# Two or four of twelve gate blocks by seven products instead of eight, in seven of nine chunks

## The chip, the cores and the metric

The kernel runs on one core of a Trainium2 chip. The metric is device time in microseconds from the first to the last instruction of the program and what lies around it. Three runs of the kernel before gave 318.49 us in the median (318.02 to 319.49). The core's engines work side by side, each through its own queue in program order: TensorE (PE), which multiplies and writes into the eight banks of PSUM; VectorE (DVE) and ScalarE (ACT), which read PSUM and SBUF; GpSimd (POOL), which here works on SBUF alone; and SyncE (SP), which issues most transfers.

## The reference

Windowed attention (8 batches, 8 heads, 576 tokens, head size 64; four heads with a plain window of 32, four with a dilated one), and behind it a block with gates:

```python
attn = softmax(where(mask[h], q @ k.T / 8, -1e9))      # per batch and head
x = (attn @ v), transposed to [8 * 576, 8 * 64]        # 4608 tokens x 512
g = x @ w_gate                                         # 512 x 1536
gelu = 0.5 * g * (1 + erf(g / sqrt(2)))
out = (gelu * (x @ w_val)) @ w_out                     # 1536 x 512
```

Inputs and output are float32.

## The kernel before

**Tiling.** The block behind the attention runs over 9 chunks of 512 tokens (`run_chunk`, c = 0 to 8). Each chunk has two stages. In the *gate stage* the 1536 middle columns are 12 blocks of 128 (nb = 0 to 11). For each block TensorE makes a gate and a value: four matmuls each (128 rows of weights from `wg` or `wv`, 512 tokens of `xT`, one for each quarter of the 512 inputs; `ffn1_part`, L622) into one bank each. ScalarE makes the Gelu of the gate bank (`g`, L905), VectorE multiplies it with the value bank into `u_all` (the word `u`, L910). In the *output stage* `u_all` is multiplied with `w_out`. There, from chunk 1 on, a 2 x 2 scheme of seven products replaces eight (`products`, L704): the 12 blocks form six pairs, `wx` holds sums of `w_out`, and `u_sums` (L665, L670, L672; the words `k`) makes sums of u on VectorE: the first sum `@0` of a pair, from the two blocks, is needed by products 7 and 5, the second sum `@1` by product 6, the third sum `@2`, in place in `u_all`, by product 3. The products run in the order 1, 7, 6, 4, 5, 2, 3, twelve matmuls of 256 columns each, on two banks; `part_out` (the words `q`, L729, L738, L742) saves a bank between two products in `snap` (two parts of `vdiag`, and `turned`), or adds a saved one and sends it to `out`.

**Attention between.** The attention of the batch that the next chunk needs is laid between the products of the output stage of chunks 0 to 6: scores S (L457), exponentials P on ScalarE (L487), masks M on VectorE (L492), denominators D, logarithm and exponential l and r on ScalarE (L584, L590; tags `lg` and `rb`), numerators N and the division X on VectorE into `xT` (L613). GpSimd turns incoming float32 rows of q, k and v into float16 (L216, L228, L253).

**Order.** Nothing is scheduled automatically: each chunk's program is a string of words that `gate_words` and `out_words` make and `run_program` reads. A number emits so many matmuls of the stage's list, `g` and `u` the Gelu and the product of a block, `k`, `q`, `S`, `M` and so on the steps above. The order of the words is the order in each engine's queue. `gate_banks` gives a block its two banks: from chunk 2 on blocks of even number have (0, 7), those of odd number (1, 4).

## Time and profile before

| | us |
|---|---|
| median of three runs | 318.49 |
| the profiled execution | 318.54 |
| its span, first to last instruction | 316.8 |
| TensorE busy | 310.3 |
| VectorE busy | 211.6 |
| ScalarE busy | 163.0 |
| GpSimd busy | 84.5 |

The chunks begin at 18.5 (0), 55.3 (1), 88.4 (2), 121.9 (3), 155.3 (4), 188.2 (5), 221.0 (6), 253.4 (7) and 283.4 us (8). A row of the chain of waits has a start, a length, and the engine, the tile and the line that the time goes to. A row of groups has the line, the engine, the operation with the tiles that it writes and reads, their shapes and how often; then the busy time and the mean in ns of one; then the idle time ahead of them and who ended it. A row of stages has the stretch, its length, and for each engine the busy time and the instructions; then the granted clock (1.00 is full), the share of the DMA engines, and GB/s.

### The profile page before, as it was taken

The page shows a single profiled execution, that of the slowest core. Times are in us where ns is not written, and L with a number is a line of the kernel's source. Part 1 is how long each engine was busy: PE and PEld are TensorE (multiplying, and loading weights), DVE is VectorE, ACT ScalarE, POOL GpSimd, SP SyncE. Part 2 cuts the span into 40 slices and gives each one's busy share as a digit, 9 for nine tenths or more (in the row PEclk, how much of TensorE's full clock was granted, in tenths as well). Part 3 has the DMA queues.
Part 4 walks back from the last instruction along what each step waited for, and adds up shares of the span by engine and source line. Part 5 has one row for each costly group of instructions (what it writes and reads, how often), then busy time and mean ns, then how long its engine had stood idle before and what let it go on. Part 6 is the DMA issues. An engine that isn't in the chain of part 4 may idle for free.

```text
span 316.8 us, 8447 instructions
## 1 busy us (share of the span) xinstructions
PE 310.3 (98%) x3489; PEld 183.8 (58%) x3489; DVE 211.6 (67%) x368; ACT 163.0 (51%) x247; POOL 84.5 (27%) x134
## 2 busy tenths in 40 slices
...
PEclk9999999999999999999999999999999999999999
...
GB/s 187 185 200 206 206 198 149 257 204 197 160 262 154 198 241 147 246 206 195 160 239 247 158 187 177 244 167 131 35 0 2 79 59 1 0 107 27 0 2 132
DMA packets 110790, 47.15 MB, mean 149 GB/s; under 512 B 83616, under 2 KB 110240, under 8 KB 110752
## 3 DMA queue, kind: packets, MB, share of 16 engines
...
q8 instruction: 27, 0.44, 0.6%
...
HBM read 37.75 MB, written 9.44 MB: 149 GB/s over the span
## 4 chain that ended last, share of the span: by engine, by line
PE 93%; DVE 2%; DMA 2%; ACT 1%; issue 0%; POOL 0%; DVEq 0%
PE ps L622 59%; PE ps L704 23%; PE ps L457 6%; PE ps L629 3%; DMA xT<-in_q_dram 2%; PE ps L377 1%; ACT P L487 1%; DVE xT L613 0%; DVE P L492 0%; PE ps L796 0%; PE ps L446 0%; PE ps L397 0%; DVE u_all L910 0%; ACT rb L590 0%; POOL band L122 0%
## 5 line engine op out<-in xcount | busy, mean ns | idle before, releaser
L905 ACT ACTIVATE g<-ps 128x512 f16<-128x512 f32 x108 | 64.4, 597 | 103.1 <-PE ps L622 100.8
L910 DVE SCALAR_TENSOR_TENSOR u_all<-g,ps 128x512 f16<-128x512 f16 x108 | 73.8, 685 | 63.6 <-PE ps L622 49.0
L622 PE MATMUL ps<-xT,wv 128*128 128x512 f16 x432 | 112.3, 379 | 0.0
L622 PE MATMUL ps<-xT,wg 128*128 128x512 f16 x432 | 111.4, 379 | 0.2 <-DMA wg<-in_moe_w_gate_dram 0.2
L622 PEld LDWEIGHTS <-wg 128*128 128x128 f16 x432 | 42.1, 98 | 50.1 <-DMA wg<-in_moe_w_gate_dram 0.2
L622 PEld LDWEIGHTS <-wv 128*128 128x128 f16 x432 | 42.3, 98 | 49.6 <-issue 0.2
L704 PEld LDWEIGHTS <-u_all 128*128 128x128 f16 x390 | 36.7, 98 | 6.5 <-issue 0.3
L704 PE MATMUL ps<-wx,ux 128*128 128x256 f16 x288 | 35.4, 273 | 0.1
L704 PE MATMUL ps<-wo,u_all 128*128 128x256 f16 (+1 forms) x294 | 35.2, 271 | 0.0
L613 DVE TENSOR_TENSOR xT<-ps,rb 128x576 f16<-128x576 f32 x32 | 29.1, 938 | 4.5 <-PE ps L457 3.6
L487 ACT ACTIVATE P<-ps 128x832 f16<-128x832 f32 (+1 forms) x32 | 25.3, 835 | 11.4 <-PE ps L457 11.3
L216 POOL CAST s<-stage 128x640 f16<-128x640 f32 x24 | 18.3, 790 | 46.1 <-DMA stage<-in_q_dram 32.5
L704 PEld LDWEIGHTS <-ux 128*128 128x128 f16 x288 | 27.7, 98 | 4.1 <-issue 0.2
L253 POOL CAST v<-stage 128x1152 f16<-128x1152 f32 x11 | 12.7, 1152 | 62.7 <-DMA stage<-in_v_dram 47.5
L665 DVE TENSOR_TENSOR ux<-u_all 128x512 f16<-128x512 f16 x48 | 24.4, 509 | 1.7
L584 ACT ACTIVATE lg<-ps 128x576 f32<-128x576 f32 x30 | 18.8, 655 | 6.9 <-PE ps L457 3.7
L590 ACT ACTIVATE rb<-lg 128x576 f32<-128x576 f32 x30 | 19.0, 688 | 0.1
L228 POOL CAST s<-stage 128x512 f16<-128x512 f32 x24 | 15.4, 670 | 9.8 <-DMA stage<-in_q_dram 8.1
L672 DVE TENSOR_TENSOR u_all<-ux,u_all 128x512 f16<-128x512 f16 (+1 forms) x32 | 13.8, 430 | 0.9
L670 DVE TENSOR_TENSOR ux<-u_all,ux 128x512 f16<-128x512 f16 (+1 forms) x32 | 13.5, 422 | 1.1
L729 DVE SCALAR_TENSOR_TENSOR part<-ps,vdiag 128x512 f32<-128x512 f32 x15 | 10.3, 688 | 3.7 <-PE ps L704 3.7
L704 PE MATMUL ps<-wx,u_all 128*128 128x256 f16 x96 | 11.8, 273 | 0.0
...
## 6 DMA issues: line engine op xcount, KB each, us to landing
...
```

What stands on the lines that cost most here:

```text
L216: nc.gpsimd.tensor_copy(s16[:, 1280 * t + 640 * g : 1280 * t + 640 * g + 640].rearrange("p (k c) -> p k c", k=5), st_of(i).rearrange("p (k ...
L228: nc.gpsimd.tensor_copy(s16[:, at : at + 512].rearrange("p (r h d) -> p h r d", r=4, h=2), st_of(i)[:, 512 * g : 512 * g + 512].rearrange( ...
L457: nc.tensor.matmul(o[cols], lhs[rows], rhs[rows], start=st, stop=end, skip_group_check=True)
L487: nc.scalar.activation(pt[:, 0 : src.shape[1]], src, AF.Exp, bias=0.0, scale=scale)
L584: nc.scalar.activation(lg, psf[:, c0 : c0 + S], AF.Ln)
L590: nc.scalar.activation(rb, tiles.pop(("lg", n)), AF.Exp, scale=-1.0)
L613: nc.vector.tensor_tensor(dst, num, rb, ALU.mult)
L622: nc.tensor.matmul(ps[:, bank, :], w[:, kc, ns], xT[kc][:, tok], start=first, stop=end)
L665: nc.vector.tensor_tensor(ux[:, j, 0:2], k0, u_all[:, 2 * j : 2 * j + 2, hi], ALU.subtract)
L704: lambda o=o, s=s[:, P * p : P * p + P], t=t[:, c0:c1], st=st, end=end: nc.tensor.matmul(o, s, t, start=st, stop=end, skip_group_check=True)
L905: nc.scalar.activation(g, ps[:, gate_banks(c, args[0])[0], :], AF.Gelu)
L910: nc.vector.scalar_tensor_tensor(u_all[:, nb, :], tiles.pop(("g", nb)), -USCALE if c in SEVEN and nb % 2 else USCALE, val, ALU.mult, ALU.mult)
```

## The change

In chunks 3 to 8 the blocks 2 and 3 (pair 1), and in chunks 7 and 8 also the blocks 4 and 5 (pair 2), are no longer made by four matmuls for each gate and value. The product of the pair's 256 weight columns with 512 tokens over 512 inputs is cut into 2 x 2 quarters of weights and of x, and made by seven products of quarters (`ffn1_seven`, the words `f`). One product has four matmuls of 256 columns: gate and value, two blocks of 128 inputs each. Gate and value share one bank, 256 columns each.

- **Sums of weights** (`gate_sums`, words `h`): four sums each for gate and value; for pair 1 in chunk 2 on VectorE, for pair 2 in chunk 6 on GpSimd. They lie in columns of x that are no longer needed.
- **Sums of x** (`x_sums`, words `x`): four of 128 x 512 per chunk; for chunks 3 to 5 on VectorE at the start of the gate stage, for 6 to 8 on GpSimd. For this `xT` becomes one tile.
- **Out of the banks** (`quarter_out`): after products 1, 6 and 7 ScalarE copies the bank into a saved one; after 2, 5 and 4 VectorE adds a saved one to the bank, into a float32 quarter of 128 x 512 (in buffers of `rb` and `lg`); after 3 ScalarE copies. Two words later ScalarE makes the Gelu of the quarter's gate half (`quarter_gelu`), and another word later VectorE the product (`quarter_u`), 128 x 256 each.
- **Places.** The products stand one by one between the half blocks of four matmuls of the direct blocks 4 to 9 (in chunks 7 and 8 those of both pairs, from block 6 on). Pair 1 uses banks 1 and 4, pair 2 banks 2 and 3. The direct blocks in between all use banks 0 and 7, in chunks 7 and 8 also 5 and 6.
- **Sums of u**, in chunks 1 to 8: the second and third sums of pair 4 are made together with those of pair 5; in the output stage of chunks 1 to 6 the third sum moves behind the first two masks. In chunks 3 to 8 pair 1's sums come late in the gate stage.

Three places on VectorE. The first is chunk 4's gate stage from its start (`ux` takes a first or second sum of u, `ps` are the banks). Before:

```order
L910 SCALAR_TENSOR_TENSOR u_all<-g,ps 128x512 x2
L665 TENSOR_TENSOR ux<-u_all 128x512
L910 SCALAR_TENSOR_TENSOR u_all<-g,ps 128x512 x2
L665 TENSOR_TENSOR ux<-u_all 128x512
L670 TENSOR_TENSOR ux<-u_all,ux 128x2x256
L672 TENSOR_TENSOR u_all<-ux,u_all 128x2x256
L910 SCALAR_TENSOR_TENSOR u_all<-g,ps 128x512 x2
```

Now:

```order
L670 TENSOR_TENSOR xT<-xT 128x512 x4
L1017 SCALAR_TENSOR_TENSOR u_all<-g,ps 128x512 x3
L709 TENSOR_TENSOR quarter<-ps,vdiag 128x512
L766 TENSOR_TENSOR ux<-u_all 128x512
L1017 SCALAR_TENSOR_TENSOR u_all<-g,ps 128x512
L766 TENSOR_TENSOR ux<-u_all 128x512
L1017 SCALAR_TENSOR_TENSOR u_all<-g,ps 128x512
L726 SCALAR_TENSOR_TENSOR u_all<-g,quarter 128x256
L709 TENSOR_TENSOR quarter<-ps,turned 128x512
L1017 SCALAR_TENSOR_TENSOR u_all<-g,ps 128x512
L709 TENSOR_TENSOR quarter<-ps,vdiag 128x512
```

Four sums of x stand ahead of the first u, and adds of banks and half-width u between the direct ones. The second place is the end of chunk 4's gate stage and the first masks. Before:

```order
L910 SCALAR_TENSOR_TENSOR u_all<-g,ps 128x512 x2
L665 TENSOR_TENSOR ux<-u_all 128x512
L670 TENSOR_TENSOR ux<-u_all,ux 128x256
L742 TENSOR_SCALAR vdiag<-ps 128x512
L672 TENSOR_TENSOR u_all<-ux,u_all 128x256
L492 TENSOR_TENSOR P_2975<-P_2975,two_p 128x832
L492 TENSOR_TENSOR P_2977<-P_2977,two_p 128x832
```

Now:

```order
L1017 SCALAR_TENSOR_TENSOR u_all<-g,ps 128x512
L771 TENSOR_TENSOR ux<-u_all,ux 128x2x256
L1017 SCALAR_TENSOR_TENSOR u_all<-g,ps 128x512
L766 TENSOR_TENSOR ux<-u_all 128x512
L771 TENSOR_TENSOR ux<-u_all,ux 128x2x256
L843 TENSOR_SCALAR vdiag<-ps 128x512
L493 TENSOR_TENSOR P_3037<-P_3037,two_p 128x832
L493 TENSOR_TENSOR P_3039<-P_3039,two_p 128x832
L773 TENSOR_TENSOR u_all<-ux,u_all 128x2x256 x2
```

A second sum (of pairs 0 and 1) stands between the last two u, the second sum ahead of the saved bank is twice as wide, and the third sums stand behind the masks. The third place is the end of chunk 7's gate stage. Before:

```order
L665 TENSOR_TENSOR ux<-u_all 128x512
L670 TENSOR_TENSOR ux<-u_all,ux 128x256
L672 TENSOR_TENSOR u_all<-ux,u_all 128x256
L910 SCALAR_TENSOR_TENSOR u_all<-g,ps 128x512 x2
L665 TENSOR_TENSOR ux<-u_all 128x512
L670 TENSOR_TENSOR ux<-u_all,ux 128x256
L672 TENSOR_TENSOR u_all<-ux,u_all 128x256
```

Now:

```order
L726 SCALAR_TENSOR_TENSOR u_all<-g,quarter 128x256 x3
L1017 SCALAR_TENSOR_TENSOR u_all<-g,ps 128x512
L726 SCALAR_TENSOR_TENSOR u_all<-g,quarter 128x256
L766 TENSOR_TENSOR ux<-u_all 128x512
L726 SCALAR_TENSOR_TENSOR u_all<-g,quarter 128x256
L766 TENSOR_TENSOR ux<-u_all 128x512 x2
L1017 SCALAR_TENSOR_TENSOR u_all<-g,ps 128x512
L771 TENSOR_TENSOR ux<-u_all,ux 128x3x256
L1017 SCALAR_TENSOR_TENSOR u_all<-g,ps 128x512
L766 TENSOR_TENSOR ux<-u_all 128x512
```

Five half-width u and two more first sums have moved in ahead of the last two u. The core of the diff:

```diff
@@ -78,7 +78,8 @@
     wg_t = [const.tile([P, NKC, b - a], F16, tag=f"wg{i}", name=f"wg{i}") for i, (a, b) in enumerate(WC)]
     wv_t = [const.tile([P, NKC, b - a], F16, tag=f"wv{i}", name=f"wv{i}") for i, (a, b) in enumerate(WC)]
     wo_t = [const.tile([P, 4, DM], F16, tag=f"wo{i}", name=f"wo{i}") for i in range(3)]
-    xT = [const.tile([P, NT], F16, tag=f"xT{i}", name=f"xT{i}") for i in range(NKC)]
+    x_all = const.tile([P, NKC, NT], F16, tag="xT", name="xT")
+    xT = [x_all[:, i] for i in range(NKC)]
 
     vraw = [const.tile([P, 4 * NB2 * D], F16, tag=f"v{i}", name=f"v{i}") for i in range(3)]
     vdiag = const.tile([P, 2 * NB2 * P], F16, tag="vdiag")
@@ -624,6 +625,106 @@
     def parts_of(order):
         return [(kc, i == 0, i == len(order) - 1) for i, kc in enumerate(order)]
 
+    ONE = ((1, (1, 4)),)
+    IN_PLACES = {c: ONE if c < 7 else ONE + ((2, (2, 3)),) for c in range(3, NCH)}
+    IN_SEVEN = {c: [j for j, _ in IN_PLACES[c]] for c in IN_PLACES}
+    sums_at = {1: 0, 2: 2 * CH, 3: 3 * CH}
+    free_pool = range(6, NCH)
+    def sums_of(j, s):
+        return x_all[:, s, sums_at[j] : sums_at[j] + CH].rearrange("p (m k n) -> p m k n", m=2, k=2)
...
+    def gate_sums(j, part):
+        for m in range(2):
+            (a11, a12), (a21, a22) = quarters(j, m)
+            s1, s2, s3, s4 = (sums_of(j, s)[:, m] for s in range(4))
+            out_, first, other, op = (
+                (s1, a21, a22, ALU.add),
+                (s2, s1, a11, ALU.subtract),
+                (s3, a11, a21, ALU.subtract),
+                (s4, a12, s2, ALU.subtract),
+            )[part]
+            (nc.vector if j == 1 else nc.gpsimd).tensor_tensor(out_, first, other, op)
+    def x_halves(c):
+        at = [slice(c * CH + 2 * P * h, c * CH + 2 * P * h + 2 * P) for h in range(2)]
+        return [[x_all[:, 2 * k : 2 * k + 2, a] for a in at] for k in range(2)]
+    def x_sum(s):
+        return x_all[:, s, CH : 2 * CH].rearrange("p (k t) -> p k t", k=2)
+    def x_sums(c):
+        (b11, b12), (b21, b22) = x_halves(c)
+        t1, t2, t3, t4 = (x_sum(s) for s in range(4))
+        for out_, first, other in ((t2, b12, b11), (t1, b22, t2), (t3, b22, b12), (t4, b21, t1)):
+            (nc.gpsimd if c in free_pool else nc.vector).tensor_tensor(out_, first, other, ALU.subtract)
+    def ffn1_seven(c, j, kind, bank, first):
+        (b11, b12), (b21, b22) = x_halves(c)
+        for m in range(2):
+            (a11, a12), (_, a22) = quarters(j, m)
+            s1, s2, s3, s4 = (sums_of(j, s)[:, m] for s in range(4))
+            left, right = {
+                1: (a11, b11),
+                2: (a12, b21),
+                3: (s4, b22),
+                4: (a22, x_sum(3)),
+                5: (s1, x_sum(1)),
+                6: (s2, x_sum(0)),
+                7: (s3, x_sum(2)),
+            }[kind]
+            for k in range(2):
+                nc.tensor.matmul(
+                    ps[:, bank, 2 * P * m : 2 * P * m + 2 * P],
+                    left[:, k],
+                    right[:, k],
+                    start=first and m == 0 and k == 0,
+                    stop=k == 1,
+                    skip_group_check=True,
+                )
+    def quarter_out(c, j, kind, bank):
+        src, kept = ps[:, bank, :], {1: 0, 6: 1, 7: 2}.get(kind)
+        saved = snap if bank in (1, 4) else [stage[:, DM * i : DM * i + DM] for i in range(3)]
+        if kept is not None:
+            nc.scalar.copy(saved[kept], src)
+            return
+        n = tiles["quarters"] = tiles.get("quarters", 0) + 1
+        t = nrm.tile([P, S], F32, tag=("rb", "lg", "rb", "lg", "rb")[n % 5], bufs=(3, 2, 3, 2, 3)[n % 5], name="quarter")[:, 0:DM]
+        if kind == 3:
+            nc.scalar.copy(t, src)
+        else:
+            nc.vector.tensor_tensor(t, src, saved[{2: 0, 4: 1, 5: 2}[kind]], ALU.add)
+        nb, half = 2 * j + (kind in (4, 5)), int(kind in (3, 5))
+        tiles.setdefault("ready", []).append((nb, half, t))
+    def quarter_gelu():
+        for nb, half, t in tiles.pop("due", []):
+            g = ffn.tile([P, 2 * P], F16, tag="gq")
+            nc.scalar.activation(g, t[:, 0 : 2 * P], AF.Gelu)
+            tiles.setdefault("gated", []).append((nb, half, t, g))
+        tiles["due"] = tiles.pop("ready", [])
+    def quarter_u():
+        for nb, half, t, g in tiles.pop("gated", []):
+            dst = u_all[:, nb, 2 * P * half : 2 * P * half + 2 * P]
+            by = -USCALE if nb % 2 else USCALE
+            nc.vector.scalar_tensor_tensor(dst, g, by, t[:, 2 * P : 4 * P], ALU.mult, ALU.mult)
...
@@ -850,6 +951,12 @@
 
         if c == 0:
             return ((4, 5), (6, 7))[nb] if nb < 2 else ((0, 1), (2, 3))[nb % 2]
+        if c in IN_SEVEN:
+            if nb in (1, 11):
+                return (1, 4)
+            if c > 6:
+                return (5, 6) if nb % 2 else (0, 7)
+            return (4, 1) if nb == 9 else (0, 7)
         return ((0, 7), (1, 6) if c == 1 else (1, 4))[nb % 2]
 
...
@@ -864,7 +971,7 @@
                 first.append((nb, gi, (kc, i == 1, i == NKC)))
         else:
             first = [(nb, gi, part) for nb in range(2) for gi in range(2) for part in parts_of(range(NKC))]
-        order = [(nb, gi) for nb in range(2, NNB) for gi in range(2)]
+        order = [(nb, gi) for nb in range(2, NNB) if nb // 2 not in IN_SEVEN.get(c, ()) for gi in range(2)]
         if c == 0:
             order = [(nb + n, gi) for nb in range(2, 10, 2) for gi in range(2) for n in range(2)] + order[16:]
         rest = [(nb, gi, part) for nb, gi in order for part in parts_of(range(NKC))]
@@ -915,6 +1022,19 @@
                 u_sums(*args)
             elif kind == "K":
                 weight_sums(*args)
+            elif kind == "f":
+                j, product, place = args
+                ffn1_seven(c, j, product, place, product in (1, 2, 7))
+                quarter_u()
+                quarter_gelu()
+                quarter_out(c, j, product, place)
...
             elif kind == "q":
                 what, eng, at = (args + [c])[:3]
                 part_out(at, what, eng, out_banks(at)[what in (1, 3, 5)])
@@ -952,21 +1072,59 @@
         sums = [""] * NNB
         if c in SEVEN:
             for j in range(NKP - 1):
-                sums[2 * j + 1] += f" k{j}@0" + (f" k{j}@1@2 k{j}@2@2" if j % 2 else " k4@1 k4@2" if j == 4 else "")
+                sums[2 * j + 1] += f" k{j}@0" + (f" k{j}@1@2 k{j}@2@2" if j % 2 else "")
         if c == min(SEVEN):
             for n, nb in enumerate((1, 2, 2, 4, 4, 4, 5, 6, 6, 8, 8, 8)):
                 sums[nb] += f" K{n // 4}@{n % 4}"
+        before = "" if c == NCH - 1 else f"q6@1@{c - 1}"
+        last = f" u{NNB - 1} k5@0 k5@1 k5@2" if c > 6 else ""
+        first = "7 G 1 g0 2 u0 4 g1 2 u1" if c < NCH - 1 else "4 g0 4 u0 4 g1 4 u1"
+        if c in IN_SEVEN:
+            words = seven_words(c)
+            loads = f"{loads} x" if c < NCH - 1 else loads
+            return f"{before} {loads} {first} {words} 4 g{NNB - 1} {BLOCKS[c][2]} 4 {BLOCKS[c][3]}"
         blocks = [f"4 g{nb} 4 u{nb}{sums[nb]}" for nb in range(2, NNB - 1)]
         if c in (1, 2):
             n = NHP * (c + 1)
             blocks[9 - c] += f" S{n}@12+S{n + 1}@{14 if c == 1 else 15}"
+        if c == 2:
+            for part in range(4):
+                blocks[2 * part + 1] += f" h1@{part}"
         rest = " ".join(blocks)
         if c == 1:
             return f"{loads} 8 G 3 g0 1 u0 3 g1 1 u1{sums[1]} {rest} 4 g{NNB - 1} 4"
-        before = "" if c == NCH - 1 else f"q6@1@{c - 1}"
-        last = f" u{NNB - 1} k5@0 k5@1 k5@2" if c > 6 else ""
-        first = "7 G 1 g0 2 u0 4 g1 2 u1" if c < NCH - 1 else "4 g0 4 u0 4 g1 4 u1"
         return f"{before} {loads} {first}{sums[1]} {rest} 4 g{NNB - 1} 4{last}"
+    one = (
+        [0, 1, 1, 0, 1, 1, 0, 1, 1, 1, 0, 0, 0, 0, 0],
+        "||k0@0||k2@0||||k3@0|k3@1@2|U k3@2@2|U|U k4@0|k1@0|k1@1@2",
+    )
+    late = "|".join(w + h for w, h in zip(one[1].split("|"), [""] * 11 + [" h2@0", " h2@1", " h2@2", " h2@3"]))
+    two = (
+        [0, 2, 2, 2, 2, 2, 2, 2, 0, 0, 0],
+        "k0@0||||k3@0|||U|U k4@0|U k1@0 k2@0|k2@1@3",
+    )
+    BLOCKS = {c: (*one, "", "") for c in range(3, 6)}
+    BLOCKS[6] = (one[0], late, "", "")
+    BLOCKS[7] = BLOCKS[8] = (*two, "", "u11 k5@0 k5@1@3 k2@2@3 k5@2@3")
+    def seven_words(c):
+        pairs = IN_PLACES[c]
+        orders = [[f"f{j}@{product}@{banks[n % 2]}" for n, product in enumerate((1, 2, 6, 7, 5, 4, 3))] for j, banks in pairs]
+        pairs = [j for j, _ in pairs]
+        groups = orders[0] if len(pairs) == 1 else [w for both in zip(*orders[:2]) for w in both]
+        direct = [nb for nb in range(2, NNB - 1) if nb // 2 not in pairs]
+        slots, after = BLOCKS[c][0], BLOCKS[c][1].split("|")
+        words = [groups.pop(0) for _ in range(slots[0])] + [after[0]]
+        for n, nb in enumerate(direct):
+            for part in range(2):
+                words.append(f"4 {'gu'[part]}{nb}")
+                for _ in range(slots[2 * n + part + 1]):
+                    words.append(groups.pop(0))
+                words.append(after[2 * n + part + 1])
+        assert not groups
+        return " ".join(words)
 
     def out_words(c):
 
@@ -976,12 +1134,13 @@
                 "w0@0 H2 N6@50+N7@20 D4@52+D5@22 X6 l5 X7 l4 r4 r5 10 N4@20+N5@40 X4 X5 2 e3@0"
             )
         if c > 6:
-            return "12 q0@1 12 q1@1 12 q2@1 12 q3@0 12 q4@0 12 q5@0 12 q6@1" if c < NCH - 1 else "L"
+            return "12 q0@1 x8 12 q1@1 12 q2@1 12 q3@0 12 q4@0 12 q5@0 12 q6@1" if c < NCH - 1 else "L"
         i, j, k, l = (NHP * (c + 1) + n for n in range(NHP))
         v0, v1 = (" v0", " v1") if 2 < c < 6 else ("", "")
+        late = "k1@2@2 " if c in IN_SEVEN else ""
         after = f"S{l + 1}@12+S{l + 2}@15" if 1 < c < 6 else ""
         return (
-            f"E P{i} P{j} 1 u11 k5@0 k5@1 11 q0@0 k5@2 M{i} M{j}{v0} 12 q1@1 8 "
+            f"E P{i} P{j} 1 u11 k5@0 k5@1@2 11 q0@0 M{i} M{j}{v0} {late}k5@2@2 12 q1@1 8 "
             f"S{k}@1+S{l}@4 D{i}@11+D{j}@41 P{k} P{l} 4 q2@0 M{k} M{l}{v1} 12 l{i} l{j} r{i} r{j} q3@0 "
             f"12 N{i}@10+N{j}@40 D{k}@12+D{l}@42 q4@0 X{i} l{l} X{j} l{k} r{l} r{k} 12 q5@0 {6 if c < 3 else 4} "
             f"N{k}@13+N{l}@43 {after} X{l} X{k} {6 if c < 3 else 8}"
```

11 lines of the change are left out of this document (added).

## The prediction

> **What bounds the kernel now.** I read the page first, then the chain of waits, then the stages. On the page the TensorE row and the row of its granted clock:
>
> ```profile
> PE 310.3 (98%) x3489; PEld 183.8 (58%) x3489; DVE 211.6 (67%) x368; ACT 163.0 (51%) x247; POOL 84.5 (27%) x134
> PEclk9999999999999999999999999999999999999999
> ```
>
> TensorE is busy for 310.3 of 316.8 us at full clock. Busy alone proves little, so the chain of waits comes next (start, length, what):
>
> ```profile
> 121.89 20.73 PE ps L622 x96
> ...
> 144.63 0.60 DVE vdiag L742
> 145.24 0.58 DVE u_all L672
> 145.81 1.13 DVE P L492 x2
> ...
> 155.32 20.72 PE ps L622 x96
> 176.04 3.49 PE ps L704 x32
> 179.54 0.87 PE ps L457 x64
> 180.40 3.16 PE ps L704 x28
> ...
> 253.44 20.79 PE ps L622 x96
> 274.23 9.17 PE ps L704 x84
> ```
>
> Except for one stretch in chunk 3 the chain is an unbroken run of matmuls. In chunk 4 (from 155.32) the gate stage is 96 matmuls of 512 columns in 20.72 us, 0.2158 us each; the output stage of chunk 7 is 84 of 256 columns in 9.17 us, 0.1092 us each. A column costs about the same in both forms, so columns taken from TensorE are time taken from the end, as long as VectorE and ScalarE keep up. Their load by stage (gate stage of chunk 2 with its output stage; gate stages of chunks 4, 6, 7):
>
> ```profile
> 88.38:121.89 33.51, 33.51 (x413) 20.06 (x412) 23.23 (x41) 18.73 (x28) 14.86 (x24) 1.00 1.27 202
> 155.32:176.04 20.72, 20.72 (x99) 9.46 (x97) 13.55 (x24) 9.26 (x15) 7.63 (x11) 1.00 0.95 236
> 221.00:241.72 20.72, 20.72 (x98) 9.44 (x97) 12.81 (x24) 9.26 (x15) 0.00 (x0) 1.00 0.05 16
> 253.44:274.23 20.79, 20.79 (x98) 9.45 (x97) 13.04 (x24) 9.05 (x14) 0.00 (x0) 1.00 0.07 23
> ```
>
> The columns after the length are PE, PEld, DVE, ACT, POOL. VectorE has 7.2 us of 20.72 free in chunk 4, ScalarE 11.5.
>
> **TensorE's part.** One pair of gate blocks costs 2 x 2 x 4 = 16 matmuls of 512 columns: 16 x 0.2158 = 3.453 us. Seven products cost 7 x 4 = 28 matmuls of 256 columns: 28 x 0.1092 = 3.058 us. Saved: 0.395 us per pair and chunk. Chunks 3 to 6 do it for one pair, 7 and 8 for two: 4 + 4 = 8 times, **3.16 us**. Nothing else on TensorE changes in number. The other price for a 256-column matmul is 3.16 / 28 = 0.1129 us (the row at 180.40); whether that applies is a rival below.
>
> **VectorE and ScalarE in a gate stage.** The prices:
>
> ```profile
> L910 DVE SCALAR_TENSOR_TENSOR u_all<-g,ps 128x512 f16<-128x512 f16 x108 | 73.8, 685 | 63.6 <-PE ps L622 49.0 <-ACT g L905 14.3
> L905 ACT ACTIVATE g<-ps 128x512 f16<-128x512 f32 x108 | 64.4, 597 | 103.1 <-PE ps L622 100.8 <-DVE wx L656 1.1 <-DVE u_all L910 1.1
> L729 DVE SCALAR_TENSOR_TENSOR part<-ps,vdiag 128x512 f32<-128x512 f32 x15 | 10.3, 688 | 3.7 <-PE ps L704 3.7
> L760 ACT ACTIVATE c<-ps 128x256 f32<-128x256 f32 x2 | 0.8, 384 | 3.9 <-PE ps L704 3.9
> L762 DVE SCALAR_TENSOR_TENSOR c<-ps,vdiag 128x256 f32<-128x256 f32 x1 | 0.4, 425 | 0.0
> 268.15 0.42 DVE L665 TENSOR_TENSOR ux<-u_all 128x512 f16<-128x512 f16 x1
> 272.07 0.29 DVE L670 TENSOR_TENSOR ux<-u_all,ux 128x256 f16<-128x256 f16 x1
> ```
>
> Chunk 4, VectorE: minus two u of 0.69 (1.37); plus three adds of a bank to a saved quarter, like L729, 2.06; plus four half-width u, like L762, 1.70; plus four sums of x at 0.42, 1.68; minus the sums of u that leave the stage (one third sum of 0.42 goes behind the masks, the two 0.29 sums of pair 4 are merged into those of pair 5), 1.0. So 13.55 becomes 16.6 of now 20.3 us. ScalarE: minus two Gelu, plus four copies of a bank at 0.60 and four half Gelu at 0.38: 9.26 + 2.7 = 12.0. Chunk 7: VectorE 13.04 - 2.74 + 4.13 + 3.40 - 1.7 = 16.1 of 19.9, ScalarE 9.05 - 2.4 + 4.8 + 3.1 = 14.5. Both fit, so what counts is the places where TensorE waits for one result.
>
> *Start of a stage.* The four sums of x stand ahead of u0. In chunk 5:
>
> ```profile
> 187.11 2.16 DVE L613 TENSOR_TENSOR xT<-ps,rb 128x576 f16<-128x576 f32 x2 [0.48 <-PE ps L457]
> 190.74 0.69 DVE L910 SCALAR_TENSOR_TENSOR u_all<-g,ps 128x512 f16<-128x512 f16 x1 [1.47 <-ACT g L905]
> ```
>
> VectorE idles 1.47 us there, and four sums in a row take some 1.8: u0 ends 0.35 us later, 3.6 us into the stage. Its bank is wanted after 16 + 4 + 4 matmuls, at 4.75. No stall; with all four stretched (below) by 0.3 it would just begin.
>
> *Middle.* Between blocks 4 to 8 the same two banks serve every block. The value bank of block 4 is wanted again 4 x 0.2158 + 4 x 0.1092 = 1.30 us after its last matmul; u needs 0.11 to start (176.15 after 176.04, below) and 0.69: slack 0.5 us. The adds and copies on the quarter banks have a slack above 1 us, since two blocks' matmuls lie between two uses of a bank. Cost zero, and it stays zero while VectorE is less than 0.5 us behind.
>
> *End.* This is the tight place. Chunk 4 on VectorE around the end of the stage at 176.04:
>
> ```profile
> 174.70 0.68 DVE L910 SCALAR_TENSOR_TENSOR u_all<-g,ps 128x512 f16<-128x512 f16 x1
> 176.15 0.69 DVE L910 SCALAR_TENSOR_TENSOR u_all<-g,ps 128x512 f16<-128x512 f16 x1 [0.77 <-PE ps L622]
> 176.87 0.42 DVE L665 TENSOR_TENSOR ux<-u_all 128x512 f16<-128x512 f16 x1
> 177.33 0.29 DVE L670 TENSOR_TENSOR ux<-u_all,ux 128x256 f16<-128x256 f16 x1
> 177.54 0.68 DVE L742 TENSOR_SCALAR vdiag<-ps 128x512 f32<-128x512 f32 x1
> 178.34 1.09 DVE L492 TENSOR_TENSOR P<-P,two_p 128x832 f16<-128x832 f16 x2
> ```
>
> L742 saves product 1 out of bank 0 and ends at +2.18; product 6 goes on in that bank after 24 matmuls, at +2.62: slack 0.44. The wider second sum of pair 5 (0.42 for 0.29) takes 0.13 of it, 0.31 stays. The third sum that leaves the place ahead of the masks gives 0.28 back to the masks, not to L742. How late is u11? From the end of block 8's value (15.1 us into the stage) to block 11's (20.4) there are 5.3 us, and VectorE has three u, three half-width u and four sums of u: 2.07 + 1.28 + 1.68 = 5.0 us. It arrives nearly without reserve, and GpSimd works there:
>
> ```profile
> 171.39 1.18 POOL L228 CAST s<-stage 128x512 f16<-128x512 f32 x2 [1.20 <-DMA stage<-in_q_dram]
> 172.88 1.44 POOL L228 CAST s<-stage 128x512 f16<-128x512 f32 x2 [0.32 <-DMA stage<-in_k_dram]
> ...
> 202.07 1.18 POOL L228 CAST s<-stage 128x512 f16<-128x512 f32 x2 [1.24 <-DMA stage<-in_q_dram]
> 203.47 1.36 POOL L228 CAST s<-stage 128x512 f16<-128x512 f32 x2 [0.23 <-DMA stage<-in_k_dram]
> ```
> ```profile
> 202.81 0.71 DVE L665 TENSOR_TENSOR ux<-u_all 128x512 f16<-128x512 f16 x1
> 203.55 0.81 DVE L670 TENSOR_TENSOR ux<-u_all,ux 128x512 f16<-128x512 f16 x1
> ```
>
> In chunk 5 sums of u that take 0.42 alone took 0.71 and 0.81 beside a cast, while u, which reads a bank and one SBUF tile, keeps a mean of 685 ns over all 108. So each sum beside a cast costs about 0.35 more. In chunk 4 the casts of 171.4 to 174.3 fall at 16.5 to 19.4 us into the new stage (it begins 0.4 earlier), on three sums of u: from none to 1.05 us. Less the reserve of 0.3 and the slack of 0.31, TensorE stalls 0 to 0.45; I take 0.2. The Trainium skill ("SBUF — State Buffer", section "Who interferes with whom") says that a VectorE instruction with two SBUF inputs and a GpSimd instruction that reads SBUF shut each other out for a whole instruction; by that the half-width u, both of whose inputs are in SBUF, would be caught too. The trace agrees for sums (0.71 against 0.42); no row of it shows a half-width u. By the rule six instructions could be caught instead of three, and the stall would be up to 1.5 us; by the row of u alone it is the 0.45 above.
>
> Chunk 5's casts end some 18 us into the new stage: 0.1. Chunk 3 has no slack already: L742 ends at 145.24, 2.62 after its stage's end at 121.89 + 20.73 = 142.62, and the masks end at 146.94, with TensorE waiting:
>
> ```profile
> 146.99 0.57 PE L457 MATMUL ps<-P,ones 64*64 64x96 f16 x26 [0.16 <-DVE P L492]
> ```
>
> The move of the third sum (0.58 in the chain above) behind the masks removes this wait of 0.16; the wider second sum holds L742 and product 6 up by 0.13, and casts add something: net +0.1, from -0.2 to +0.9.
>
> Chunk 7 and 8: GpSimd has little to do, but between block 8's and block 11's end (6.9 us) VectorE has three u, two adds, six half-width u and four sums, 2.06 + 1.38 + 2.55 + 1.8 = 7.8 us: u11 is 0.9 late at most (the durations overlap a little back to back: 174.70 follows a 0.29 row that began at 174.49). Product 7 needs the first sum of pair 5 for its last two matmuls, at +2.40; before, it was there at +1.25 (176.87 + 0.42 in chunk 4, the same here). Slack 1.15, so 0 to 0.3 each; I take 0.05 each.
>
> **On GpSimd and before chunk 3.** The eight weight sums of pair 1 (8 x 0.29 = 2.3 us) lie in chunk 2, where VectorE is busy 23.23 of 33.51 us and two pairs of banks alternate: 0. The sums of x in chunks 6 to 8 and of pair 2's weights go to GpSimd, idle in the rows of chunks 6 and 7. Nearest rows:
>
> ```profile
> L216 POOL CAST s<-stage 128x640 f16<-128x640 f32 x24 | 18.3, 790 | 46.1 <-DMA stage<-in_q_dram 32.5 <-DMA stage<-in_k_dram 13.6
> ```
>
> One sum takes 0.6 by its size, or up to 1.6 if a second input costs as much again and more. The second of four, which product 6 needs first, is ready 2.3 to 4.3 us into the stage, and product 6 starts at 7.8 (28 matmuls of 512 columns and 16 of 256 stand ahead of it). Hidden either way.
>
> **Sum.** The profiled execution took 318.54 us (span 316.8 and 1.74 around it), 0.05 above the median of 318.49. 318.54 - 3.16 + 0.2 + 0.1 + 0.1 + 0.1 = **315.9 us**. With no stall at all and chunk 3's wait gone: 318.54 - 3.16 - 0.2 = 315.2.
>
> **Rivals.** *Late ends* (0.20): VectorE comes late at most stage ends, because the half-width u are caught by casts too and ScalarE's half Gelu arrive late. Chunk 4 at 0.7, chunk 3 at 0.7, chunk 5 at 0.3, chunks 7 and 8 at 0.3: 318.54 - 3.16 + 2.3 = 317.7, range 316.6 to 318.3. For: 5.0 of 5.3 us and 7.8 of 6.9. Against: in chunk 4 only one of three sums in 171 to 175 was stretched.
>
> *Edges* (0.05, the slower side): each run of four products between blocks costs what runs between the attention units cost. 28 matmuls there took 3.16, not 3.06: 0.10 per run. 7 runs x 8 pairs = 56 runs, 5.6 us: 318.54 - 3.16 + 5.6 = 321.0. It decides from 0.056 per run. Against: at 176.04 and 274.23 512-column matmuls turn into 256-column ones and the rows are 32 x 0.109 = 3.49 and 9.17, with no edge; the 0.10 goes with the 64-row matmuls of L457.
>
> *VectorE as the bound of chunks 3 to 5* (0.03, slower): if GpSimd shut VectorE out for all of its 7.63 us in chunk 4, 16.6 + 7.6 is 3.9 over 20.3; at some 2 to 2.4 in chunks 3 and 5 with fewer casts that is 8 us, 323. It decides from half of GpSimd's time on; the rows above show a third or less. It is what the lock in the Trainium skill ("SBUF — State Buffer", "Who interferes with whom") would give if the cast always came first.
>
> *The saving doesn't arrive* (0.04), about 318.5, for a wait I have not seen.
>
> **How the numbers follow.** Forecast 0.68 (315.2 to 316.5), late ends 0.20, no saving 0.04, slower 0.08. A measurement here can tell about 0.5%, 1.6 us: faster means below 316.9. That holds for the forecast and a quarter of the late ends: 0.73; same 0.19; slower 0.08. The range 315.0 to 317.7 holds the forecast and most of the late ends.
>
> **What would show it.** Gate stages of 20.3 us (chunks 3 to 6) and 19.9 (7, 8) in the chain, with 28 products of 0.109 us each; VectorE near 16.6 of 20.3 in chunk 4; waits of TensorE only for L742's successor or the sums of u in chunks 3 to 5, below 0.5 us each. Wrong if products cost 0.113 or more, if value matmuls of blocks 5 to 8 wait for u, or if the stages of chunks 7 and 8 end in a wait above 0.5 us.

## The result: 0.68% faster, and the profile after

The changed kernel took 316.71 us in the median of six executions (316.46 to 316.99), the kernel before on the same chip 318.93 us (318.02 to 319.49). The ratio is 0.9932, with a 95% interval from 0.9915 to 0.9949: faster by 2.2 us. (The gate blocks are made by sevens in chunks 3 to 8, which are six of the nine chunks and not seven as the title has it.) The profiled execution took 316.73 us, its span fell from 316.8 to 315.0. The gate stages gave what they should; about half of it was spent again in output stages, more than half of that in the one of chunk 4.

The page's rows of engines, after:

```profile
PE 308.0 (98%) x3585; PEld 193.2 (61%) x3585; DVE 227.7 (72%) x408; ACT 179.5 (57%) x295; POOL 104.4 (33%) x154
```

TensorE lost 2.3 us of busy time, VectorE gained 16, ScalarE 16, GpSimd 20. The stages one by one, after (length; then busy time of PE, PEld, DVE, ACT, POOL with the instructions): gate and output stage of chunk 3, gate and output stage of chunk 4, gate stages of chunks 7 and 8.

```profile
122.08:142.42 20.34, 20.34 (x110) 10.65 (x109) 15.84 (x29) 11.32 (x21) 5.25 (x6) 1.00 0.81 212
142.42:155.25 12.83, 12.31 (x293) 10.35 (x292) 10.69 (x17) 9.40 (x14) 3.42 (x6) 1.00 0.99 179
155.25:175.58 20.33, 20.33 (x110) 10.65 (x109) 15.70 (x30) 11.32 (x21) 7.57 (x11) 1.00 0.96 236
175.58:188.61 13.03, 12.44 (x293) 10.29 (x292) 10.61 (x19) 9.41 (x14) 2.46 (x2) 1.00 0.61 163
253.09:273.09 20.00, 20.00 (x122) 11.80 (x121) 15.11 (x27) 13.29 (x26) 8.27 (x7) 1.00 0.07 24
282.38:302.31 19.93, 19.93 (x122) 11.79 (x121) 13.17 (x27) 11.90 (x25) 0.00 (x0) 1.00 0.08 27
```

In each gate stage TensorE is busy for the whole length. In the output stages of chunks 3 and 4 it is idle for 0.52 and 0.59 us. Here is where the span went, stage by stage, in the first profile of each kernel (us; one row for chunks 3 to 6, since they are alike, and output stages that differ by no more than 0.02 are left out):

| | before | after | difference |
|---|---|---|---|
| before chunk 1's gate stage | 55.3 | 55.0 | -0.29 |
| output of chunk 1 | 11.78 | 12.14 | +0.36 |
| output of chunk 2 | 12.22 | 12.34 | +0.12 |
| gate of chunks 3 to 6, each | 20.72 | 20.33 | -0.38 to -0.40, together -1.57 |
| output of chunk 3 | 12.71 | 12.85 | +0.14 |
| output of chunk 4 | 12.13 | 13.04 | +0.91 |
| gate of chunk 7 | 20.79 | 20.00 | -0.79 |
| output of chunk 7 | 9.17 | 9.29 | +0.12 |
| gate of chunk 8 | 20.72 | 19.93 | -0.79 |

Together -1.8: the gate stages gained 3.15 and the output stages gave back 1.65. Of the 0.29 ahead of chunk 1, 0.23 is a wait of the kernel before in chunk 0 (number 607 in *The wait that nothing releases*), and not the change. The chain of waits of after shows the two places in chunks 3 and 4 (start, length, what):

```profile
142.51 0.70 DVE u_all L1017
143.23 0.77 DVE ux L766
144.02 0.86 DVE ux L771
144.89 0.61 DVE vdiag L843
145.54 1.03 PE ps L805 x8
...
175.63 0.40 issue
176.03 0.70 DVE u_all L1017
176.75 0.44 DVE ux L766
177.21 0.42 DVE ux L771
177.63 0.61 DVE vdiag L843
178.29 1.03 PE ps L805 x8
...
186.96 0.49 issue
```

In both chunks the way goes from the last u (L1017) over the first and second sums of u (L766, L771) to the saved bank (L843), and TensorE goes on behind it. "issue" is time in which an engine waited for nothing that the profile shows. It appears twice in chunk 4: VectorE starts the last u 0.40 us late, and near the end of the stage TensorE stands still for 0.49 us ahead of its last score matmul (L458). The table of TensorE's waits, after (how long in all, how often, the longest):

```profile
PE ps L805 <- DVE vdiag L843: 0.5, 1, 0.5
PE ps L458 <- issue: 0.5, 1, 0.5
...
PE ps L458 <- DVE P L493: 0.2, 1, 0.2
```

Such a row counts idle time, which is less than what the wait costs: a matmul of 256 columns is shown with 0.27 us here, while the next one starts 0.11 us later, so the first 0.16 us of a wait still count as busy. From start to start, less the usual distance, the wait for the saved bank (L843) was 0.69 us in chunk 3 and 0.26 in chunk 4, where the table has no row for it, and the wait ahead of the score matmul 0.67. The two in chunk 4 make 0.93, the whole of its 0.91.

The last row belongs to chunk 1, whose output stage is 0.36 longer. There two masks on VectorE, and GpSimd's cast of v beside them, after:

```profile
78.43 1.15 POOL L254 CAST v<-stage 128x1152 f16<-128x1152 f32 x1 [2.66 <-DMA stage<-in_v_dram]
...
78.54 1.92 DVE L493 TENSOR_TENSOR P<-P,two_d 128x768 f16<-128x768 f16 x2
```

and before, where the cast had begun at 78.17 and was over when these masks came:

```profile
79.38 1.01 DVE L492 TENSOR_TENSOR P<-P,two_d 128x768 f16<-128x768 f16 x2
```

Two masks of two SBUF inputs each took 1.92 us beside the cast and 1.01 alone. Whether they meet depends on when the input arrives.

### The profile page after: what moved, and what is told of

The parts are those of the page before. It is cut to its first block, busy times and chain, and to the rows that moved or that the text cites. A ratio compares the mean times of both kernels' runs of the same rounds, so it can differ in the third digit from the quotient of the medians.

```text
span 315.0 us, 8745 instructions
## 1 busy us (share of the span) xinstructions
PE 308.0 (98%) x3585; PEld 193.2 (61%) x3585; DVE 227.7 (72%) x408; ACT 179.5 (57%) x295; POOL 104.4 (33%) x154
## 4 chain that ended last, share of the span: by engine, by line
PE 88%; DVE 5%; DMA 4%; POOL 1%; issue 1%; ACT 0%; DVEq 0%
PE ps L623 49%; PE ps L805 21%; PE ps L688 8%; PE ps L458 6%; PE ps L730 3%; DMA wg<-in_moe_w_gate_dram 2%; DMA xT<-in_q_dram 2%; DVE u_all L1017 1%; DVE ux L766 1%; DVE ux L771 1%; DVE P L493 1%; DVE vdiag L843 1%; DVE u_all L726 0%; POOL xT L182 0%; PE ps L378 0%
## 5 line engine op out<-in xcount | busy, mean ns | idle before, releaser
L1012 ACT ACTIVATE g<-ps 128x512 f16<-128x512 f32 x92 | 54.8, 597 | 78.8 <-PE ps L623 78.7
L1017 DVE SCALAR_TENSOR_TENSOR u_all<-g,ps 128x512 f16<-128x512 f16 x92 | 63.0, 685 | 49.9 <-PE ps L623 33.3
L623 PE MATMUL ps<-xT,wv 128*128 128x512 f16 x368 | 95.8, 379 | 0.0
L623 PE MATMUL ps<-xT,wg 128*128 128x512 f16 x368 | 95.0, 379 | 0.2
L623 PEld LDWEIGHTS <-wg 128*128 128x128 f16 x368 | 35.8, 98 | 38.7 <-DMA wg<-in_moe_w_gate_dram 0.2
L623 PEld LDWEIGHTS <-wv 128*128 128x128 f16 x368 | 36.0, 98 | 37.0 <-DMA wv<-in_moe_w_val_dram 0.4
L670 POOL TENSOR_TENSOR xT<-xT 128x512 f16<-128x512 f16 x12 | 13.9, 1182 | 33.0 <-DVE xT L614 25.4
L766 DVE TENSOR_TENSOR ux<-u_all 128x512 f16<-128x512 f16 x48 | 22.4, 478 | 0.8
L688 PE MATMUL ps<-xT 128*128 128x256 f16 x128 | 17.9, 273 | 0.0
L726 DVE SCALAR_TENSOR_TENSOR u_all<-g,quarter 128x256 f16<-128x256 f16 x32 | 15.8, 497 | 1.8 <-ACT g L717 1.8
L688 PEld LDWEIGHTS <-xT 128*128 128x128 f16 x128 | 12.5, 98 | 6.6
```

The lines of the kernel that those rows point to most:

```text
L623: nc.tensor.matmul(ps[:, bank, :], w[:, kc, ns], xT[kc][:, tok], start=first, stop=end)
L688: nc.tensor.matmul(ps[:, bank, 2 * P * m : 2 * P * m + 2 * P], left[:, k], right[:, k], start=first and m == 0 and k == 0, stop=k == 1, sk ...
L766: nc.vector.tensor_tensor(ux[:, j, 0:2], k0, u_all[:, 2 * j : 2 * j + 2, hi], ALU.subtract)
L1012: nc.scalar.activation(g, ps[:, gate_banks(c, args[0])[0], :], AF.Gelu)
L1017: nc.vector.scalar_tensor_tensor(u_all[:, nb, :], tiles.pop(("g", nb)), -USCALE if c in SEVEN and nb % 2 else USCALE, val, ALU.mult, ALU.mult)
```

## The experiments

My theory was that the saving on TensorE is real and complete, and that what is missing is waits at the starts of output stages: work on VectorE that stands ahead of the saved bank, lengthened by casts. One rival was that the placing of the sums, not the sevens, moves the time; another that the differences between output stages are chance of single executions; a third, for the 0.49 us without a releaser, that something belongs to the place in the program. Ratios are to the kernel before, timed on the same chip, with 95% intervals.

### The same kernels again

No edit, for the changed kernel and then for the one before.

> The changed kernel once more, unchanged, for a second trace. Theory (waits at the end of gate stages): TensorE waits for L843 in chunk 3 by 0.4 to 0.6 us again, chunk 1 is 33.3 to 33.5 us long because its two masks meet a cast, gate stages are 20.33 us; span 314.8 to 315.2. Rival (chance): what chunk 1 and chunk 4 lost in the first trace (0.37 and 0.51 us, 0.49 of it a wait of TensorE that no instruction ends) is not there again; span 314.2 to 314.6, chunk 4 at most 32.7 us.

> The kernel before once more, for a second trace. Theory: chunk 1 takes 33.0 to 33.1 us again, since its masks stand behind the third sum and miss the cast; span 316.7 to 317.0. Rival (chance): chunk 1 takes 33.4 us in this trace too, or the span differs by over 0.5 us.

Measured: the changed kernel 0.9931 (0.9904 to 0.9958), 316.38 us against 319.15; span 313.8. The kernel before in a second profile: 319.03 us, span 317.3.

The gate stages came out the same to 0.01 us in both, but for chunk 4's in the repetition (20.38, where the gate of block 11 waited 0.06 for a u). The output stages didn't. After again: chunk 1 11.82, chunk 3 12.29 (its wait for L843 down from 0.69 to 0.18), chunk 4 12.37. Before again: chunk 1 12.25, chunk 2 12.90, chunk 3 12.11. So of what I expected of the first run only the gate stages came true: chunk 1 took 33.1 us, not 33.3 to 33.5, and chunk 3's wait wasn't 0.4 to 0.6. In the second run chunk 1 took 33.5 us, as the rival of chance had it. Its waits of TensorE hold a row for masks:

```profile
PE ps L457 <- DVE P L492: 0.4, 1, 0.4
```

So output stages of chunks 1 to 3 vary by 0.5 to 0.7 us in the *kernel before* as well, and the differences of +0.36, +0.12 and +0.14 above can't be put down to the change. The chain of the repeated run, chunk 4:

```profile
175.12 0.40 issue
175.51 0.70 DVE u_all L1017
...
177.12 0.61 DVE vdiag L843
```

The late start of the last u came again at the same instruction with the same 0.40, and the wait for the saved bank behind it with the same 0.26; TensorE's 0.49 near the stage's end didn't.

Chunk 3 shows what changed between the two runs. VectorE and GpSimd, after:

```profile
142.54 1.17 POOL L229 CAST s<-stage 128x512 f16<-128x512 f32 x2 [0.52 <-DMA stage<-in_q_dram]
144.00 1.36 POOL L229 CAST s<-stage 128x512 f16<-128x512 f32 x2 [0.28 <-DMA stage<-in_k_dram]
...
143.23 0.76 DVE L766 TENSOR_TENSOR ux<-u_all 128x512 f16<-128x512 f16 x1
144.02 0.86 DVE L771 TENSOR_TENSOR ux<-u_all,ux 128x512 f16<-128x512 f16 x1
```

and in the repetition:

```profile
140.51 2.82 POOL L229 CAST s<-stage 128x512 f16<-128x512 f32 x4 [0.40 <-DMA stage<-in_q_dram]
...
143.49 0.42 DVE L766 TENSOR_TENSOR ux<-u_all 128x512 f16<-128x512 f16 x1
143.94 0.42 DVE L771 TENSOR_TENSOR ux<-u_all,ux 128x512 f16<-128x512 f16 x1
```

0.76 and 0.86 beside the casts, 0.42 and 0.42 with the casts over: 0.78 us on the way to the saved bank, and a wait of 0.52 for TensorE.

### Only the placing of the sums, no sevens

```diff
-    IN_PLACES = {c: ONE if c < 7 else ONE + ((2, (2, 3)),) for c in range(3, NCH)}
+    IN_PLACES = {c: ONE if c < 7 else ONE + ((2, (2, 3)),) for c in ()}
...
-        last = f" u{NNB - 1} k5@0 k5@1 k5@2" if c > 6 else ""
+        last = f" u{NNB - 1} k5@0 k5@1@2 k5@2@2" if c > 6 else ""
...
-                blocks[2 * part + 1] += f" h1@{part}"
+                pass
...
-            return "12 q0@1 x8 12 q1@1 12 q2@1 12 q3@0 12 q4@0 12 q5@0 12 q6@1" if c < NCH - 1 else "L"
+            return "12 q0@1 12 q1@1 12 q2@1 12 q3@0 12 q4@0 12 q5@0 12 q6@1" if c < NCH - 1 else "L"
```

> The kernel after without the seven products of the gate stage: no products, sums of x or sums of weights for them; x in one tile, the merged sums of pairs 4 and 5 and the third sums behind the masks stay. Theory: chunk 1 loses 0.2 to 0.4 us against before, chunk 3 stays within 0.2; time 0 to 0.4 us above before (ratio 1.000 to 1.0015). Rival (the moved sums help): 0.2 to 0.6 us below before, since chunk 3's wait for the masks goes.

Measured: 0.9987 (0.9962 to 1.0012), 318.85 us. It can't be told from the kernel before. Its gate stages are back at 20.72. In this profile the wide second sum ahead of the saved bank cost TensorE two waits, one in chunk 1 and one in chunk 2:

```profile
PE ps L805 <- DVE vdiag L843: 1.2, 2, 0.6
```

So the gain comes with the sevens, and the new order of the sums, with the wide second sum ahead of the saved bank, is no gain by itself.

### Sevens in chunks 3 to 6 alone

```diff
-    IN_PLACES = {c: ONE if c < 7 else ONE + ((2, (2, 3)),) for c in range(3, NCH)}
+    IN_PLACES = {c: ONE if c < 7 else ONE + ((2, (2, 3)),) for c in range(3, 7)}
...
-    BLOCKS = {c: (*one, "", "") for c in range(3, 6)}
-    BLOCKS[6] = (one[0], late, "", "")
+    BLOCKS = {c: (*one, "", "") for c in range(3, 7)}
```

The lines for the sums of u at the end of chunks 7 and 8 and for the sums of x on GpSimd change as in the version without sevens. Chunks 7 and 8 then have their eight products again, with the merged sums of pairs 4 and 5.

> The kernel after with the seven products in chunks 3 to 6 alone; chunks 7 and 8 make all their blocks directly, without sums of x and weights for them. Theory: four of eight savings of 0.395 us go, so 1.4 to 1.6 us above the kernel after, ratio to before 0.997 to 0.9985. Rival (chunks 7 and 8 give most of their saving back at the ends of their gate stages): less than 0.8 us above the kernel after.

Measured: 0.9988 (0.9969 to 1.0007), 318.55 us; 0.57% above the full change as run again, 1.8 us. The gate stages of chunks 7 and 8 took 20.80 and 20.72, the output stage of chunk 7 9.17. The expected 1.4 to 1.6 were the two gate stages' 0.79 each less the 0.12 in the output stage; the time came out about so. The gate stages of 3 to 6 kept their 20.32, yet half of the change shows no gain that can be told: its 1.57 us are spent elsewhere, in this profile 1.17 in chunk 4's output stage (13.30, 12.13 before) and 0.55 ahead of chunk 1's gate stage.

### Third sums ahead of the masks again

```diff
-            f"E P{i} P{j} 1 u11 k5@0 k5@1@2 11 q0@0 M{i} M{j}{v0} {late}k5@2@2 12 q1@1 8 "
+            f"E P{i} P{j} 1 u11 k5@0 k5@1@2 11 q0@0 {late}k5@2@2 M{i} M{j}{v0} 12 q1@1 8 "
```

> The kernel after with one part undone: in the output stage of chunks 1 to 6 the third sums (of pairs 4 and 5, and of pairs 0 and 1 in chunks 3 to 6) stand ahead of the two masks again, behind the saved bank. Theory: chunk 1 gets back some of its loss if its masks miss the cast (33.0 to 33.2 us); in chunks 3 to 6 the masks come 0.42 to 0.84 us later and TensorE waits for them by 0.2 to 0.9 us each; together 0.5 to 2 us above the kernel after. Rival (the masks have slack enough): the same time as the kernel after, within 0.3.

Measured: 0.9981 (0.9966 to 0.9995), 318.5 us: 0.49% above the change, 1.6 us, and its interval lies wholly above the change's (0.9915 to 0.9949). The output stages took 12.56 in chunk 1, 13.40 in chunk 3, 12.37 in 5 and 11.98 in 6. Chunks 5 and 6, which hardly vary in the other runs (12.10 to 12.12 and 11.72), rise by 0.26 each. Moving the third sums behind the masks is therefore a part of the change that the sevens need: with pair 1's sums in this place, the masks come too late.

### The saved bank ahead of the second sums

The opposite edit takes work away from in front of the saved bank. The second sums now stand behind the masks too (first version) or between the saved bank and the masks (second):

```diff
-            f"E P{i} P{j} 1 u11 k5@0 k5@1@2 11 q0@0 M{i} M{j}{v0} {late}k5@2@2 12 q1@1 8 "
+            f"E P{i} P{j} 1 u11 k5@0 11 q0@0 M{i} M{j}{v0} k5@1@2 {late}k5@2@2 12 q1@1 8 "
```

> The kernel after with the saved bank of product 1 (L843) and the two masks ahead of the second sum of pairs 4 and 5 on VectorE, in chunks 1 to 6; nothing else. Theory (L843 behind the wide second sum makes TensorE wait): the wait of 0.52 us in chunk 3 goes, and that of about 0.3 in chunk 4; the second sum is needed only by the last four matmuls of product 6, behind the scores and denominators; 0.6 to 1.0 us below the kernel after, ratio to before 0.990 to 0.9915. Rival (VectorE late at the end of the gate stage is the cause): the wait in chunk 3 shrinks by less than 0.3 us.

```diff
+            f"E P{i} P{j} 1 u11 k5@0 11 q0@0 k5@1@2 M{i} M{j}{v0} {late}k5@2@2 12 q1@1 8 "
```

> The kernel after with the saved bank of product 1 (L843) ahead of the second sum of pairs 4 and 5, but the masks behind that sum. Theory: the wait for L843 goes as in the run with masks first; the masks end as in the kernel after, so chunk 1's loss stays; 0.5 to 0.9 us below the kernel after. If this is faster than the run with masks first, earlier masks are worth nothing or meet more casts.

Measured: the first 0.9903 (0.9886 to 0.9921), 315.80 us; the second 0.9941 (0.9919 to 0.9963), 317.14 us. In the first, chunk 3's output stage is 12.11, and of all waits in the table behind the start of the program one is left, 0.2 us ahead of L458 without a releaser. VectorE in chunk 3 of this version:

```profile
143.42 0.65 DVE L766 TENSOR_TENSOR ux<-u_all 128x512 f16<-128x512 f16 x1
144.00 0.68 DVE L843 TENSOR_SCALAR vdiag<-ps 128x512 f32<-128x512 f32 x1
144.60 1.60 DVE L493 TENSOR_TENSOR P<-P,two_p 128x832 f16<-128x832 f16 x2
```

A cast still lies on these rows (0.65 for the sum, 1.60 for the masks), but the saved bank is done at 144.68, 2.09 us into the output stage, where it was 3.10 in after, and TensorE doesn't notice. The second version sends the wait to the masks:

```profile
PE ps L458 <- DVE P L493: 0.7, 2, 0.5
PE ps L458 <- issue: 0.5, 1, 0.5
```

So the saved bank alone ahead of the second sum isn't enough; masks alone ahead of it were not tried. That the wait for L843 came from what stands ahead of it on VectorE is shown by all profiles together: each of the five with the wide second sum ahead of the bank (after, the repetition, without sevens, sevens in chunks 3 to 6, third sums ahead) has two or three such waits of 0.18 to 0.94 us from start to start, and of the seven with the bank ahead (these two and the five that follow) one has a single wait of 0.13 and six have none. The first version is 0.9 us below the change by the ratios, though the two intervals overlap a little (0.9915 to 0.9921). The following versions are built on it.

### Chunk 7 and chunk 8: two small causes

The half-width u ran beside GpSimd's sums of x in chunk 7, and the last pair of product 7 waited there. Two edits take these away one by one: chunk 8's sums of x on VectorE, and the first sum of pair 5 ahead of the second sum of pairs 0 to 2.

```diff
-    free_pool = range(6, NCH)
+    free_pool = range(6, NCH - 1)
...
-            loads = f"{loads} x" if c < NCH - 1 else loads
+            loads = f"{loads} x"
...
-            return "12 q0@1 x8 12 q1@1 12 q2@1 12 q3@0 12 q4@0 12 q5@0 12 q6@1" if c < NCH - 1 else "L"
+            return "12 q0@1 12 q1@1 12 q2@1 12 q3@0 12 q4@0 12 q5@0 12 q6@1" if c < NCH - 1 else "L"
```

> save_first with the four sums of x for chunk 8 on VectorE at the start of chunk 8, instead of on GpSimd in chunk 7; nothing else. Theory (a VectorE instruction with two SBUF inputs and a GpSimd instruction that reads SBUF shut each other out): the three half-width u in a row of chunk 7 that took 2.41 us beside GpSimd's sums take 1.1 to 1.3; VectorE ends its gate stage earlier and the 0.11 us that product 7 of chunk 7 waits for the first sum of pair 5 stay or go; time within 0.3 of save_first. Rival (half-width u are slow for another reason): they keep 0.8 each.

```diff
-        "k0@0||||k3@0|||U|U k4@0|U k1@0 k2@0|k2@1@3",
+        "k0@0||||k3@0|||U|U k4@0|U k1@0 k2@0|",
...
-    BLOCKS[7] = BLOCKS[8] = (*two, "", "u11 k5@0 k5@1@3 k2@2@3 k5@2@3")
+    BLOCKS[7] = BLOCKS[8] = (*two, "", "u11 k5@0 k2@1@3 k5@1@3 k2@2@3 k5@2@3")
```

> save_first with the second sum of pairs 0 to 2 behind the first sum of pair 5 on VectorE in chunks 7 and 8, instead of ahead of the last u. Theory (product 7's last two matmuls wait for the first sum of pair 5): the output stages of chunks 7 and 8 go from 9.29 to 9.17 us; time 0.1 to 0.3 below save_first, too little to tell. Rival: product 6 then waits for the second sum instead, and they stay at 9.29 or grow.

Measured: 0.9899 (0.9866 to 0.9932), 315.74 us, and 0.9898 (0.9858 to 0.9938), 316.33 us. Either edit alone brings the output stage of chunk 7 from 9.29 to 9.17, as before the change; 0.12 us is too little for the medians. Chunk 8's output stage had lost nothing (12.69 in before, after and both of these), so what I expected of it didn't come. The cause is in the rows of VectorE and GpSimd. After, chunk 7:

```profile
265.38 4.98 POOL L670 TENSOR_TENSOR xT<-xT 128x512 f16<-128x512 f16 x4 [7.46 <-PE ps L688]
...
268.57 2.41 DVE L726 SCALAR_TENSOR_TENSOR u_all<-g,quarter 128x256 f16<-128x256 f16 x3
```

and with chunk 8's sums on VectorE, the half-width u in the same stage:

```profile
266.63 0.41 DVE L726 SCALAR_TENSOR_TENSOR u_all<-g,quarter 128x256 f16<-128x256 f16 x1
...
267.56 0.89 DVE L726 SCALAR_TENSOR_TENSOR u_all<-g,quarter 128x256 f16<-128x256 f16 x2
```

0.80 each beside GpSimd, 0.41 to 0.45 without it.

All three edits together:

> The three changes of order together on the kernel after: bank saved and masks ahead of the second sum in chunks 1 to 6, chunk 8's sums of x on VectorE, and the first sum of pair 5 ahead of the second sum of pairs 0 to 2 in chunks 7 and 8. Theory: no wait for a saved bank in chunks 3 and 4, output stages of chunks 5 to 8 of 12.11, 11.72, 9.17 and 9.17 us; ratio to before 0.988 to 0.991, 0.8 to 1.3 us below the kernel after. Rival (the waits only move to other executions and places): ratio 0.992 or above.

Measured: 0.9894 (0.9868 to 0.9920), 316.07 us against 319.57. The output stages of chunks 5 to 7 are the expected 12.11, 11.72 and 9.17, and no wait for a saved bank or for a sum is left. The one wait without a releaser stands where it stood, and longer:

```profile
186.94 0.19 PE L458 MATMUL ps<-q 64*64 64x64 f16 x1 [0.80 <-issue]
```

By its ratio this is the fastest version, 1.06% below the kernel before, but it can't be told from the version with the saved bank first alone.

### The wait that nothing releases

It stood ahead of the *same* instruction, the last score matmul of chunk 4, in six of the nine profiles of kernels whose TensorE program has the same number of instructions up to there: 0.49 (after), 0.74 (sevens in chunks 3 to 6), 0.21, 0.47, 0.61 and 0.80 us idle. From start to start, where 0.003 us is usual in this group of matmuls, the same matmul is also late in two more, by 0.23 (third sums ahead) and 0.11 (chunk 8's sums on VectorE); in the repetition alone it isn't. Neither profile of before has this wait, nor the one without sevens. Two kernels move that instruction in TensorE's program. The first has 16 more warming matmuls at the start, which with their weight loads make 32 more instructions, on top of the version with the saved bank first:

```diff
-    warm(69, 7, 32, 32)
+    warm(85, 7, 32, 32)
```

> The kernel with the bank saved and masked first (save_first) and 16 more warm-up matmuls of 32 columns at the start, while TensorE waits for the first data: all its later instructions stand 32 places further on in its program. Theory (in chunk 4 TensorE waits for its own instructions to arrive, at a fixed place in its program): the wait of 0.4 to 0.9 us at the last score matmul of chunk 4 is gone from there; it stands 32 instructions earlier, or is hidden. Rival (something at that step of the program, such as data or a bank, holds it): it stays at the last score matmul of chunk 4. The time is that of save_first within 0.5.

The second has eight matmuls of 160 columns into a free bank in chunk 2's gate stage, 16 instructions, on top of the version with all three edits:

```diff
-                blocks[2 * part + 1] += f" h1@{part}"
+                blocks[2 * part + 1] += f" h1@{part}" + (" W8@3@1" if part == 1 else "")
```

> all_three with eight more matmuls of 160 columns on a free bank in chunk 2's gate stage: from there on TensorE's instructions stand 16 places further on. Theory (TensorE waits for instructions at a fixed place of its program): if chunk 4's output stage has the wait without a semaphore again, it stands 16 instructions (8 matmuls) ahead of the last score matmul, or not in this stage. Rival (the step of the program holds it): it stands at the last score matmul. Time 0.5 to 0.7 us above all_three, since the added matmuls take some 8 x 0.07 us.

Measured: the first 0.9949 (0.9911 to 0.9986). Its ten executions fall into two groups: four with a granted clock of 0.998 to 1.000 took 315.4 to 317.9 us, six with 0.989 took 318.9 to 321.8. The profiled one is of the second group. In its profile the wait is gone from chunk 4 (12.11) and every output stage from chunk 1 on is at or near its smallest: 11.82, 12.11, 12.21, 12.11, 12.11, 11.72. What it lost lies at the start, where chunk 0 begins at 22.54, and at 18.59 in the version without the 16 matmuls. A wait and the row of the granted clock (40 slices of 7.9 us, in tenths):

```profile
PE ps L378 <- DMA xT<-in_q_dram: 1.6, 1, 1.6
...
PEclk9789999999999999999999999999999999999999
```

The wait was 0.3 there, so it accounts for some 1.2 of the 4.0 us. The other 2.7 go with the clock: in this trace it is granted at 0.50 from 11.72 to 18.55 us, and from 6.6 us on it is full in every other trace until the last 1.5 us. Why it falls isn't shown; it does so behind the wait. The second kernel: 0.9921 (0.9895 to 0.9947), 316.82 us, of which the eight matmuls account for 0.55 (chunk 2's gate stage took 21.85 instead of 21.29). The wait is there:

```profile
187.37 0.27 PE L458 MATMUL ps<-q 64*64 64x96 f16 x9 [0.74 <-issue]
```

It stands eight matmuls earlier in the order of the work than in the kernel without the added eight, so at the same place counted from the program's start. In the first kernel the matmul at that place wasn't late.

The traces hold more of this, for both engines. TensorE first. Counted from 0 from the program's start, the late matmul of chunk 4 is number 2398 in the nine kernels above and in the second of the two moved ones. In all fourteen traces a score matmul that follows another one starts 0.18 us or more behind it, without a result of another engine or a transfer to wait for, at this number and two others alone. One is 607, in chunk 0: 0.18 to 0.40 us in nine of the fourteen profiles, both of before among them. The first of the moved kernels is another of the nine (0.28), and there number 607 stands 16 matmuls earlier in the order of the work than in the rest. The other is 1503, in chunk 2 of the version with the first sum of pair 5 ahead (0.59). These numbers are 896 and 895 apart, seven times 128 within one. Each page also has a DMA queue for instructions, here after's:

```profile
q8 instruction: 28, 0.46, 0.7%
```

Each of the 28 packets has 16384 bytes. Together that is 64.0 bytes for each of TensorE's 7170 matmuls and weight loads, so a packet is as much as 128 matmuls with their weight loads. In 17 of these 18 waits the late matmul started 1.2 to 1.6 us after the end of such a packet, in one 1.9. In the repetition number 2398 started 1.5 us after one, in its turn.

VectorE's 0.40 ahead of u11 goes with a number too. I took, for each of its instructions, the time from the end of the instruction ahead or of the last semaphore that it waits for to its start. Behind the first 6 us this is at most 0.06 us in all fourteen traces, but for the numbers 191 and 319 of VectorE's program (all instructions counted from 0, those that only wait among them), 128 apart, where it is up to 0.42. Number 319 is u11 of chunk 4 in all kernels with sevens there. In the version without sevens it is a u in chunk 5's gate stage, and that one is 0.25 late; number 191 is a u in chunk 2 and 0.40 to 0.42 late in ten of the eleven profiles of kernels with sevens.

What is shown: these waits go with a place in the engine's own program and not with the work that stands there, on TensorE they come in some executions and not in others, on VectorE nearly always where it is free in time, and no semaphore ends them. That TensorE's instructions themselves come late is the reading that fits the spacing and the packets, but no run moved a packet alone. What VectorE waits for stays open.

## Why the prediction was right, and where it wasn't

The sum said 315.9 us, from 315.0 to 317.7; the time was 316.71. That is 0.2 above the stretch of the forecast itself (315.2 to 316.5) and within that of *late ends* (316.6 to 318.3), so the total can't choose between the two; the stages can. The gain was forecast as 2.6 us against the profiled execution of before and was 2.2 between the medians, 1.8 between the profiled executions' times.

- **TensorE's part, 3.16 us: right.** Chunks 3 to 6 lost 0.38 to 0.40 each (0.395 forecast), chunks 7 and 8 0.79 each, 3.15 together. One product in the chain of after, and the direct matmuls behind it:

```profile
134.62 0.44 PE ps L688 x4
135.06 0.86 PE ps L623 x4
```

  Four matmuls take 0.44, 0.109 each, and four of 512 columns 0.86. The *edges* rival (0.10 more per run of four) fell with this.
- **Load of VectorE and ScalarE: right that both fit, somewhat too high.** Chunk 4: 15.70 and 11.32 against 16.6 and 12.0; chunk 7: 15.11 and 13.29 against 16.1 and 14.5. *VectorE as the bound* fell too: no value matmul of the blocks 5 to 8 waits for a u in any profile (the one wait of a gate stage for a u was 0.06 us, for block 11, in the repetition).
- **Start of a stage: right.** The four sums of x took 1.56 us (1.8 forecast), and TensorE did not wait.
- **GpSimd: right.** One of its sums took 1182 ns (0.6 to 1.6 forecast), hidden:

```profile
L670 POOL TENSOR_TENSOR xT<-xT 128x512 f16<-128x512 f16 x12 | 13.9, 1182 | 33.0 <-DVE xT L614 25.4
L726 DVE SCALAR_TENSOR_TENSOR u_all<-g,quarter 128x256 f16<-128x256 f16 x32 | 15.8, 497 | 1.8 <-ACT g L717 1.8
```

- **Half-width u, priced like L762 at 425 ns: too low, but it cost little.** The second row has a mean of 497 over 32: 0.42 alone, 0.80 beside GpSimd. This is what the rule in the Trainium skill ("SBUF — State Buffer", section "Who interferes with whom") says: an instruction of VectorE with two SBUF inputs and one of GpSimd that reads SBUF exclude each other. The run with chunk 8's sums on VectorE agrees, 2.41 us for three becoming 0.41 to 0.45 each. The rule would have allowed a stall of up to 1.5 us in chunk 4; the wait for the saved bank there was 0.26, and had another cause (next point).
- **Chunk 4, 0.2 forecast, +0.91 measured: the term that was mis-sized.** 0.26 of it is the wait for the saved bank (two matmuls start 0.37 us apart there, where 0.11 is usual), near the forecast. But u11 was not late by the way forecast, casts on top of 5.0 us of work in 5.3. After, GpSimd's casts and u11, whose value bank was full at 175.58:

```profile
170.58 2.90 POOL L229 CAST s<-stage 128x512 f16<-128x512 f32 x4 [1.14 <-DMA stage<-in_q_dram]
...
176.03 0.69 DVE L1017 SCALAR_TENSOR_TENSOR u_all<-g,ps 128x512 f16<-128x512 f16 x1 [0.41 <-PE ps L623]
```

  The casts were over at 173.5 and VectorE was free at 175.62, yet it began 0.40 late, in both profiles of the change alike: the wait at number 319 of VectorE's program. That the size of this part came out as forecast is luck. The way forecast exists too; the version with the saved bank first shows it in the same chunk, where the stage ended at 175.03:

```profile
173.03 1.57 DVE L766 TENSOR_TENSOR ux<-u_all 128x512 f16<-128x512 f16 x2
...
175.83 0.67 DVE L1017 SCALAR_TENSOR_TENSOR u_all<-g,ps 128x512 f16<-128x512 f16 x1
```

  Two first sums took 1.57 instead of the 0.75 in after, VectorE had no gap behind them, and u11 began 0.80 after the stage's end; TensorE waited only 0.13 for the bank, since the second sum no longer stood ahead of it. The rest of the 0.91 is TensorE's wait without a releaser, 0.67 from start to start, which the prediction didn't have. The step that failed is the assumption that only results of other engines can hold an engine up: both parts of chunk 4's loss go with places in the engines' own programs, and nothing of the 0.91 is left for casts.
- **Chunk 3, net +0.1 from -0.2 to +0.9: right.** +0.14 in the first profiles: the wait for the masks of 0.16 is gone, and one for the saved bank of 0.52 (0.69 from start to start) has come with two sums stretched by casts. It is just over the 0.5 that was set as the limit of such a wait. Two stages (12.85 and 12.29 after, 12.71 and 12.11 before) show how far chance goes.
- **Chunk 5 at 0.1, chunks 7 and 8 at 0.05 each: nearly right.** Chunk 5 0; chunk 7 +0.12, with the wait of product 7 that was named; chunk 8 0.
- **What the prediction took for fixed:** chunks 1 and 2. They lost 0.48 in the first profiles, 0.2 of it to the masks that met the cast of v, but gained on the kernel before in the second ones (12.14 and 11.82 against 11.78 and 12.25 in chunk 1). So far as the runs show, that is chance of arrival. The base was too low by 0.4: 318.54 stood for the kernel before, whose median over six is 318.93.
- ***Late ends*** (317.7) was wrong as a mechanism for the whole. Only chunk 4 lost as much as it allowed, and by another way; chunks 3, 5, 7 and 8 didn't.
